# An attention and SoLU kernel on one core: the beginning re-ordered, with a mask from one-input operations and mask products of its own

## The chip, the cores and the metric

The kernel runs on one core of one Trainium2 chip. A core has TensorE (PE, matrix products into PSUM), VectorE (DVE), ScalarE (ACT) and GpSimd (POOL) as compute engines, SyncE (SP) as a queue that issues most transfers, and 16 DMA engines. The metric is the device time of one execution in microseconds, and the median over several runs is compared.

## The reference, cut to what matters

Block-sparse attention (4 batches, 8 heads, 768 tokens, 64 per head; blocks of 32, so 24 blocks) followed by a layer with a SoLU activation:

```python
scores = q @ k.T / sqrt(64)
mask = (|blk_i - blk_j| <= 1) | first and last block row and column
mask[block qb, block kb] = True  for kb in sampled_blocks[qb]      # 3 per row
attn = softmax(where(mask, scores, -1e9))
x = (attn @ v) as [3072 tokens, 512]
h = x @ w_in                                                      # 512 -> 1024
s = h * softmax(h)
out = ((s - mean(s)) / sqrt(var(s) + 1e-6) * g_ln) @ w_out        # 1024 -> 512
```

All inputs are float32 (the block numbers are int64).

## The kernel before, in words

**Units and passes.** The attention goes in 12 passes: 4 batches times 3 thirds of the queries (256 queries each). A pass has 12 units, for 4 head pairs times 3 thirds of the keys, 144 units in all. Unit s: `scores` (L357, products L364) writes keys x queries of two heads into a PSUM tile of two banks (pool `p_sco`, two buffers); `exps` (L371) is one ACT exponential of 128x1024 out of it; `outs` (L379, products L388) multiplies with V, with a column of ones for the sum; after the third unit of a pair `normalise` (L395) divides on VectorE into `xb`. Nothing is masked after the product: K and Q carry 24 extra rows below their 64. In KT they hold `selT`, a one where the key lies in that block; in QT they hold the mask row `row_q`, minus 30000 where the query may not see that block. So one product of 88 rows gives the masked score. `mask_rows` (L589) copies these rows into KT or QT for a head pair (24x1536).

**Preparation.** q, k and v come in as float32 (`load`, L296, a staging pool by size: whole pieces, the first two chunks of a Q, its last four chunks with four buffers). `cast` (L311) makes bfloat16, `turn_mm` (L320) transposes on PE, `turn_out` (L333) copies out of PSUM into KT or QT. Batch 0 is prepared while its first pass runs: K whole, Q only its first two chunks (the first pass), then V, then the other four chunks of Q.

**The mask.** VectorE compares the block numbers with an iota, one-input for the first sample (L564), two-input for the others, which take the maximum with the one before (L567), and multiplies with a static mask that six GpSimd selects have made (L544), again two-input (L569). A product with `selT` (L578) spreads it over 768 queries; ACT copies it into the rows of head pair 0 in QT, and `mask_rows` from there into the others.

**The layer.** Of each pass's result, `x_turn` (L411) sends `xb` through a transposing transfer on SP; for each of two 128-token tiles `h_mms` (L416) makes h, `e_exp` (L425) the exponential, `solu`, `stats` and `rstd` the rest, `ln_turn` (L444) a second transposing transfer, `o_mms` (L476) the product with `w_cen_sb`, `scaled` and `store` the output. `w_cen_sb` is w_out times g_ln (`prep_w`, L659, GpSimd) less its column mean (`prep_mean`, L666, products on PE; `prep_cen`, L675, VectorE).

**The order** is written by hand. Everything before the first units is emitted as it stands; the rest goes on a plan, `at(when, fn, ...)`, sorted by `when`, whose integer part is the unit. Every engine and every queue then takes its instructions strictly in the order emitted, and waits at each for what it needs. So `at(15.9, ...)` puts a product on PE between the scores of units 17 and 18; it does not start it at a time. `zeros` (L551) emits products of a zero tile, fillers whose result nobody reads: 8 before the mask, 5 around the transposes, 12 between the first units.

Of the kernel before, what the change touches and what calls it, by code (L numbers as in the profile page):

```python
# [201 lines left out]
def kernel(  # L202
# [68 lines left out]
    w_out_f = fix.tile([128, KF, d_model], FP32, name="w_out_f")  # L271
# [24 lines left out]
    def load(eng, src, b, pr, key, c0=0, c1=NCH):  # L296
        st = a_st.tile([TQ, 2, (c1 - c0) * D], FP32, tag=f"st{c1 - c0}", name=f"st_{key}{b}_{pr}",
                       bufs={NCH: 7, 2: 4, 4: 4}[c1 - c0])
        stage[key, b, pr, c0] = st
        eng.dma_start(  # L300
            out=st.rearrange("p h (c d) -> p h c d", d=D),
            in_=src[b, 2 * pr : 2 * pr + 2].rearrange("h (p c) d -> p h c d", c=NCH)[
                :, :, c0:c1, :])
# [16 lines left out]
    def turn_mm(b, pr, key, pool, c0=0, c1=NCH):  # L320
# [3 lines left out]
        elif pool is p_op:  # L324
            tp = p_op.tile([128, 1024], BF16, tag="op", name=f"tp_{key}{b}_{pr}_{c0}")
        else:
# [29 lines left out]

    def scores(s):  # L357
        ps, b, j, pr, u = unit(s)
        sco = p_sco.tile([TQ, 2, 512], FP32, tag="sco", name=f"sco{s}")
        sco_of[s] = sco  # L360
        for hh in range(2):
            h = 2 * pr + hh
            for kk in range(2):
                nc.tensor.matmul(  # L364
                    sco[:, hh, kk * QW : (kk + 1) * QW],
                    KT[b % 2][0:KR, h * NCH + 2 * u + kk, :],
                    QT[b % 2][0:KR, h * NCH + PC * j : h * NCH + PC * (j + 1), :].rearrange(
                        "p c t -> p (c t)"),
                    start=(kk == 0), stop=(kk == 1))
# [136 lines left out]
    DVE2 = (nc.vector, nc.vector)  # L506

    with tc.manual_schedule():
# [7 lines left out]
        for pr in (1, 2):  # L516
            load(nc.sync, k, 0, pr, "k")
            load(nc.sync, q, 0, pr, "q", 0, 2)
        load(nc.sync, k, 0, 3, "k")
# [4 lines left out]
        stat_m = fix.tile([NB, NB], FP32, name="stat_m")  # L524
        nc.vector.memset(stat_m, 0.0)
        selT = fix.tile([NB, NCH, TQ], BF16, name="selT")
        nc.vector.memset(selT, 1.0)
        mask_l = fix.tile([NB, KR], BF16, name="mask_l")
        nc.vector.memset(mask_l, 0.0)
        for t in VA:  # L530
            nc.vector.memset(t[:, :, :, D : D + 1], 1.0)
# [7 lines left out]
        for fill, base, cm, step in (  # L539
            (NEG, 1, -1, 1), (NEG, 1, 1, -1),  # L540
            (0.0, -1, 1, 0), (0.0, NB - 2, -1, 0),
            (0.0, -1, 0, 1), (0.0, NB - 2, 0, -1),
        ):
            nc.gpsimd.affine_select(out=stat_m, in_=stat_m, compare_op=ALU.is_ge, fill=fill,  # L544
                                    base=base, channel_multiplier=cm, pattern=[[step, NB]])
# [5 lines left out]
        def zeros(n, pool=p_o):  # L551
# [3 lines left out]
            for _ in range(n):  # L555
# [3 lines left out]
        zeros(8)  # L559
# [3 lines left out]
        acc = [fix.tile([NB, NB], FP32, name=f"acc{r}") for r in range(NR)]  # L563
        nc.vector.tensor_scalar(out=acc[0], in0=io_f, scalar1=samp_f[:, 0:1], scalar2=None,  # L564
                                op0=ALU.is_equal)
        for r in range(1, NR):
            nc.vector.scalar_tensor_tensor(out=acc[r], in0=io_f, scalar=samp_f[:, r : r + 1],  # L567
                                           in1=acc[r - 1], op0=ALU.is_equal, op1=ALU.max)
        nc.vector.scalar_tensor_tensor(out=mask_l[:, D:KR], in0=acc[-1], scalar=0.0, in1=stat_m,  # L569
                                       op0=ALU.is_equal, op1=ALU.mult)  # L570
        cast(nc.scalar, 0, 0, "k", 0, 2, 0)
        cast(nc.scalar, 0, 0, "k", 2, NCH, 0)
        cast(nc.scalar, 0, 0, "q", 0, 2, 0)
        turn_mm(0, 0, "k", p_h, 0, 2)
        m_ps = p_sco.tile([TQ, 2, 512], FP32, tag="sco", name="m_ps")
        sel_f = selT.rearrange("p c t -> p (c t)")
        for i in range(2):
            nc.tensor.matmul(m_ps[0:KR, i, 0 : S // 2], mask_l,  # L578
                             sel_f[:, i * (S // 2) : (i + 1) * (S // 2)], start=True, stop=True)
# [4 lines left out]
        def spread(x, n):  # L584
            return x.rearrange("p (o c) -> p o c", o=1).broadcast_to([NB, n, S])

        row_q = QT[0][D:KR, 0:NCH, :].rearrange("p c t -> p (c t)")

        def mask_rows(eng, t, h0):  # L589
            eng.tensor_copy(out=rows(t, h0, h0 + 2),  # L590
                            in_=spread(sel_f if t in KT else row_q, 2))

        mask_rows(nc.gpsimd, KT[0], 2)
        mask_rows(nc.vector, KT[0], 0)
        warm_t = p_sco.tile([128, 2, 512], FP32, tag="sco", name="warm_t")[:, 0, :]
        zeros(1, warm_t)
        turn_mm(0, 0, "k", p_op, 2, NCH)
        zeros(1, warm_t)
        turn_out(0, 0, "k", DVE2, 0, 2)
        for hh in range(2):  # L600
            nc.scalar.copy(
                out=rows(QT[0], hh, hh + 1).rearrange("p o (i c) -> p (o i) c", i=2),
                in_=m_ps[D:KR, :, 0 : S // 2])
        turn_mm(0, 0, "q", p_o, 0, 2)
        zeros(3, warm_t)
        turn_out(0, 0, "q", DVE2, 0, 2)
        turn_out(0, 0, "k", DVE2, 2, NCH)
        mask_rows(nc.vector, QT[0], 2)
        cast(nc.gpsimd, 0, 1, "k")
        cast(nc.gpsimd, 0, 1, "q", 0, 2)  # L610
        scores(0)
        turn_mm(0, 1, "k", p_h)
        scores(1)
        turn_mm(0, 1, "q", p_o, 0, 2)
        turn_out(0, 1, "k", DVE2)
        turn_out(0, 1, "q", DVE2, 0, 2)

# [5 lines left out]
        load(nc.sync, q, 0, 3, "q", 0, 2)  # L623
        load(nc.sync, v, 0, 0, "v")
        for pr in range(1, NP):
            load(nc.sync, v, 0, pr, "v")
        for pr in range(NP):
            at(0.1, load, nc.sync, q, 0, pr, "q", 2, NCH)
# [340 lines left out]
```

## Time and profile before

| what | us |
|---|---|
| median of three runs | 229.55 (227.93 to 232.82) |
| the profiled execution, its own time | 228.12 |
| its span, first to last instruction | 226.1 |
| PE busy | 208.3 (92%) |
| ACT busy | 174.9 (77%) |
| DVE busy | 156.7 (69%) |
| POOL busy | 109.9 (49%) |
| first exponential starts | 10.98 |
| exponential of the second pass's first unit | 25.73 |

The profile is of one execution. Its rows of a timeline give the start, the busy time of all that is merged in the row, the engine, the line of the code, the operation with output and input, the count (x8), and in brackets how long the engine had been idle and what ended that. The mean granted clock of TensorE over the span is 0.991.

### The profile page before, as it was taken

How to read it: one execution, taken by the hardware profiler on the slowest of the kernel's cores; microseconds unless marked ns; L12 is line 12 of the kernel's file. 1: busy time of each engine (PE TensorE's matmuls, PEld its weight loads, DVE VectorE, ACT ScalarE, POOL GpSimd, SP SyncE). 2: the span in 40 equal slices, each digit the busy share in tenths (PEclk: the TensorE clock that was granted, in tenths of full speed). 3: DMA queues.
4: the chain of work that ended last, by engine and by line, in shares of the span. 5: the costliest groups of instructions: out<-in, count | busy, mean ns of one | idle time of the engine just before them, and what ended most of it. 6: DMA issues, size and time to landing. Idle time of an engine off the chain costs nothing.

```text
span 226.1 us, 5902 instructions
## 1 busy us (share of the span) xinstructions
PE 208.3 (92%) x2336; PEld 146.3 (65%) x2375; DVE 156.7 (69%) x355; ACT 174.9 (77%) x205; POOL 109.9 (49%) x152
## 2 busy tenths in 40 slices
PE   6897888979989999999999999999999999999990
PEld 2466775747757667677776766866766676665450
DVE  7797674797877756867865675786775558558780
ACT  4387888677875988987988898798798889876560
POOL 7899976255895333675853516729720000000010
PEclk9999999999999999999999999999999999999996
DMA  6999694429999329949539749659631463327312
GB/s 176 360 331 296 143 260 162 76 38 252 338 190 284 89 67 188 348 65 286 167 74 299 166 77 316 143 49 324 143 96 34 109 96 96 61 78 130 94 46 101
DMA packets 56147, 37.59 MB, mean 166 GB/s; under 512 B 38068, under 2 KB 51636, under 8 KB 56116
## 3 DMA queue, kind: packets, MB, share of 16 engines
q1 hardware_dynamic: 55172, 35.60, 61.2%
q0 software_dynamic: 528, 1.05, 2.5%
q10 hardware_dynamic: 416, 0.52, 0.7%
q8 instruction: 20, 0.33, 0.6%
q14 instruction: 11, 0.09, 0.2%
HBM read 23.07 MB, written 6.29 MB: 130 GB/s over the span
## 4 chain that ended last, share of the span: by engine, by line
PE 74%; DVE 13%; DMA 4%; ACT 3%; issue 2%; POOL 1%; SPq 0%; DVEq 0%; POOLq 0%; ACTq 0%
PE sco L364 24%; PE o L481 14%; PE op L388 14%; PE h L421 14%; DMA xT<-xb 4%; PE tp_q L329 2%; PE tp_k L329 2%; DVE KT L309 1%; DVE w_cen_sb L676 1%; DVE xb L402 1%; ACT exs L375 1%; ACT e L430 1%; DVE stats L456 1%; PE warm_t L556 1%; DVE QT L309 1%
## 5 line engine op out<-in xcount | busy, mean ns | idle before, releaser
L375 ACT ACTIVATE exs<-sco 128x1024 bf16<-128x1024 f32 x144 | 141.7, 1025 | 16.1 <-PE sco L364 13.5
L364 PE MATMUL sco<-QT,KT 88*128 88x256 bf16 x576 | 86.9, 272 | 2.2 <-ACT exs L375 1.4
L364 PEld LDWEIGHTS <-KT 88*128 88x128 bf16 x576 | 55.0, 97 | 33.2 <-issue 6.5
L388 PE MATMUL op<-VA,exs 128*128 128x65 bf16 x1152 | 52.0, 194 | 1.7 <-DVE xb L402 1.6
L388 PEld LDWEIGHTS <-exs 128*128 128x128 bf16 x1152 | 48.8, 97 | 5.2 <-issue 1.4
L421 PE MATMUL h<-w_in_sb,xT 128*128 128x512 bf16 x153 | 49.4, 378 | 2.3 <-DMA xT<-xb 1.4
L474 POOL TENSOR_TENSOR rstd<-vpe,mhalf 128x1 f32<-128x1 f32 x24 | 13.4, 560 | 71.0 <-DVE vpe L472 59.7
L481 PE MATMUL o<-w_cen_sb,lnT 128*128 128x512 bf16 x162 | 43.5, 379 | 2.2 <-DVE pt_q L338 1.4
L430 ACT ACTIVATE e<-h 128x1024 bf16<-128x1024 f32 x22 | 22.5, 1024 | 19.2 <-PE h L421 14.9
L309 POOL COPY KT<-pt_k 64x768 bf16<-64x768 bf16 x24 | 20.1, 836 | 22.3 <-DVE pt_k L338 21.6
L401 DVE RECIPROCAL recip_all<-op 128x4 f32<-128x4 f32 x48 | 8.7, 182 | 30.2 <-PE op L388 29.9
L456 DVE BATCH_NORM_STATS2 stats<-solu 128x6 f32<-128x512 bf16 x46 | 29.4, 680 | 0.0
L442 DVE TENSOR_TENSOR solu<-h,e 128x1024 bf16<-128x1024 f32 x22 | 26.7, 1216 | 1.2 <-ACT e L430 1.2
L481 PEld LDWEIGHTS <-lnT 128*128 128x128 bf16 x176 | 15.8, 97 | 15.1 <-issue 1.5
L309 POOL COPY QT<-pt_q 64x768 bf16<-64x768 bf16 x24 | 20.1, 837 | 5.5 <-DVE pt_q L338 4.1
L492 DVE TENSOR_SCALAR ot<-o,rstd 128x512 f32<-128x512 f32 x20 | 15.0, 751 | 11.0 <-issue 6.8
L402 DVE TENSOR_TENSOR xb<-op,recip_all 128x256 bf16<-128x256 f32 x48 | 20.4, 425 | 1.7
L421 PEld LDWEIGHTS <-xT 128*128 128x128 bf16 x176 | 15.7, 97 | 6.0 <-DMA xT<-xb 2.0
L309 POOL CAST qn<-st_q 128x768 bf16<-128x768 f32 (+2 forms) x19 | 14.0, 748 | 3.1 <-DMA st_q<-in_q_dram 2.8
L309 POOL CAST kn<-st_k 128x768 bf16<-128x768 f32 x15 | 12.7, 846 | 3.1 <-DMA st_k<-in_k_dram 2.3
L338 DVE COPY pt_q<-tp_q 128x768 bf16<-128x768 bf16 x12 | 6.7, 556 | 8.2 <-PE tp_q L329 8.2
L309 POOL CAST VA<-st_v 128x768 bf16<-128x768 f32 x13 | 10.9, 853 | 1.9 <-DMA st_v<-in_v_dram 1.8
(92 smaller groups left out, 156.6 us busy)
## 6 DMA issues: line engine op xcount, KB each, us to landing
st_v<-in_v_dram SPq DMA_DIRECT2D x16, 384.0 KB, 5.8
out_dram<-ot SPq DMA_DIRECT2D x23, 256.0 KB, 3.7
st_k<-in_k_dram SPq DMA_DIRECT2D x15, 384.0 KB, 4.9
st_q<-in_q_dram SPq DMA_DIRECT2D x12, 384.0 KB, 5.0
w_out_f<-in_moe_w_out_dram SPq DMA_DIRECT2D x4, 512.0 KB, 7.8
st_q<-in_q_dram SPq DMA_DIRECT2D x4, 256.0 KB, 6.9
w_in_sb<-in_moe_w_in_dram POOLq DMA_DIRECT2D x1, 1024.0 KB, 13.4
st_q<-in_q_dram SPq DMA_DIRECT2D x4, 128.0 KB, 4.6
```

The costliest lines, as they stand in the source:

```text
L309: eng.tensor_copy(out=o, in_=i)
L364: nc.tensor.matmul(sco[:, hh, kk * QW : (kk + 1) * QW], KT[b % 2][0:KR, h * NCH + 2 * u + kk, :], QT[b % 2][0:KR, h * NCH + PC * j : h * N ...
L375: nc.scalar.activation(out=exs_of[ps, pr][:, u].rearrange("p a b c -> p (a b c)"), in_=sco_of.pop(s).rearrange("p a b -> p (a b)"), func=A ...
L388: nc.tensor.matmul(op[:, hh, ic, :], exs[:, u, hh, kk, ic * TQ : (ic + 1) * TQ], VA[b % 2][:, 2 * pr + hh, 2 * u + kk, :], start=(u == 0 a ...
L402: nc.vector.tensor_tensor(out=xb_of[ps][:, :, 2 * pr * D : 2 * (pr + 1) * D].rearrange("p c (h d) -> p h c d", h=2), in0=op[:, :, :, 0:D], ...
L421: nc.tensor.matmul(h_of[ps, i][:, half, :], xT_of[ps][:, i * KD + c, :], w_in_sb[:, c, half * HF : (half + 1) * HF], start=(c == 0), stop= ...
L430: nc.scalar.activation(out=o, in_=h, func=ACT.Exp, scale=1.0, accum_out=esum_all[:, t : t + 1])
L442: nc.vector.tensor_mul(out=so, in0=h, in1=e)
L456: nc.vector.bn_stats(out=stat_of[ps, i][:, half, :], in_=so[:, half, :])
L474: nc.gpsimd.tensor_tensor(out=rstd_of[ps, i], in0=vpe, in1=mhalf, op=ALU.pow)
L481: nc.tensor.matmul(ops_of[ps, i], lnT_of[ps, i][:, c, :], w_cen_sb[:, c, :], start=(c == 0), stop=(c == KF - 1), skip_group_check=True)
L492: nc.vector.tensor_scalar(out=o, in0=i_, scalar1=r, scalar2=None, op0=ALU.mult)
```

## The change

It rewrites the beginning of the kernel, up to the layer of the second pass.

- The mask: the three comparisons each go with one input into a column of `seen` (24x24x5), whose other two columns are the neighbours (two GpSimd selects) and the first and last block (memsets); a maximum over the five columns, then one product with a per-row factor, again with one tensor input, gives `mask_l`. `row_q` becomes a tile of its own, copied by VectorE out of PSUM in two parts (256, then 512 columns).
- Units 0 to 5 (head pairs 0 and 1 of the first pass): the mask is added by four products of 24 rows (`mask_mms`) into the score tile, and `scores` uses 64 rows there. The mask rows of these pairs are copied later, before the passes that need them, all on VectorE; those of pair 2 in KT go to GpSimd.
- The first casts and transposes: the last four chunks of K of pair 0 are cast by GpSimd, Q's copy out of PSUM goes to ACT; K of pair 1 goes in two parts.
- w_in comes as four float32 loads on SP, and is cast by GpSimd (before: one load on GpSimd's queue that casts on the way). w_out then loads into the same tile, so after those casts. The last four chunks of Q of pair 0 are loaded ahead of V of pair 3, and their staging pool has three buffers.
- The fillers: 6 at first, then 2.
- `outs` of the first pass come one unit later for each pair; the layer of pass 0 two units later and that of pass 1 one unit later, the second tile of both with its h products closer together; the mean products in two steps instead of four; `prep_cen` alternates between VectorE and GpSimd; batch 1 has its own lists of when to load, cast and turn.

```diff
-                       bufs={NCH: 7, 2: 4, 4: 4}[c1 - c0])
+                       bufs={NCH: 7, 2: 4, 4: 3}[c1 - c0])
...
+    def mask_mms(s):
+        ps, b, j, pr, u = unit(s)
+        sco_of[s] = p_sco.tile([TQ, 2, 512], FP32, tag="sco", name=f"sco{s}")
+        for kk in range(2):
+            for hh in range(2):
+                nc.tensor.matmul(
+                    sco_of[s][:, hh, kk * QW : (kk + 1) * QW], selT[:, 2 * u + kk, :],
+                    row_q[:, j * QW : (j + 1) * QW],
+                    start=(kk == 0), stop=False, skip_group_check=True)
...
-        for r in range(1, NR):
-            nc.vector.scalar_tensor_tensor(out=acc[r], in0=io_f, scalar=samp_f[:, r : r + 1],
-                                           in1=acc[r - 1], op0=ALU.is_equal, op1=ALU.max)
-        nc.vector.scalar_tensor_tensor(out=mask_l[:, D:KR], in0=acc[-1], scalar=0.0, in1=stat_m,
-                                       op0=ALU.is_equal, op1=ALU.mult)
+        for r in range(NR):
+            nc.vector.tensor_scalar(out=seen[:, :, r], in0=io_f,
+                                    scalar1=samp_f[:, r : r + 1], scalar2=None,
+                                    op0=ALU.is_equal)
+        any_f = fix.tile([NB, NB], FP32, name="any_f")
+        nc.vector.reduce_max(out=any_f, in_=seen, axis=AX.X)
+        mask_l = fix.tile([NB, NB], BF16, name="mask_l")
+        nc.vector.tensor_scalar(out=mask_l, in0=any_f, scalar1=0.0, scalar2=neg_r,
+                                op0=ALU.is_equal, op1=ALU.mult)
...
         cast(nc.scalar, 0, 0, "k", 0, 2, 0)
-        cast(nc.scalar, 0, 0, "k", 2, NCH, 0)
         cast(nc.scalar, 0, 0, "q", 0, 2, 0)
+        cast(nc.gpsimd, 0, 0, "k", 2, NCH, 0)
...
+        row_mm(0, 0, QW)
+        turn_mm(0, 0, "k", p_o, 0, 2)
         turn_out(0, 0, "k", DVE2, 0, 2)
...
+        turn_mm(0, 0, "q", p_op, 0, 2)
+        turn_out(0, 0, "q", ACT2, 0, 2)
+        mask_mms(0)
+        row_mm(1, QW, S)
+        turn_mm(0, 0, "k", p_sco, 2, NCH)
         turn_out(0, 0, "k", DVE2, 2, NCH)
+        mask_rows(nc.gpsimd, KT[0], 4)
+        scores(0)
...
+        mask_mms(1)
         scores(1)
...
+        for eng, when, t, h0 in (
+            (nc.vector, 0.9, QT[0], 4), (nc.vector, 3.8, KT[0], 6), (nc.vector, 3.85, QT[0], 6),
+            (nc.vector, 7.5, KT[0], 0), (nc.vector, 7.9, QT[0], 0),
+            (nc.vector, 10.0, KT[0], 2), (nc.vector, 11.2, QT[0], 2),
+            (nc.gpsimd, 14.5, KT[1], 0), (nc.vector, 15.4, QT[1], 0),
+            (nc.vector, 16.6, KT[1], 2), (nc.vector, 18.3, QT[1], 2),
+            (nc.vector, 19.9, KT[1], 4), (nc.vector, 21.3, QT[1], 4),
+            (nc.vector, 30.4, KT[1], 6), (nc.vector, 33.4, QT[1], 6),
+        ):
+            at(when, mask_rows, eng, t, h0)
...
-        for n in range(4):
-            at(n + 0.9, zeros, 3, p_op)
+        at(4.9, zeros, 2, p_op)
...
-            nc.gpsimd.dma_start(out=w_in_sb, in_=moe_w_in.rearrange("(c p) f -> p c f", p=128))
+            nc.sync.dma_start(out=w_f[:, c, :], in_=moe_w_in[c * 128 : (c + 1) * 128, :])
...
-        at(2.25, w_load_in)
-        at(9.0, w_load_out, 0, 6)
-        at(12.1, w_load_out, 6, KF)
...
+        for c in range(KD):
+            at(0.2, w_load_in, c)
+            at(12.0 + 0.1 * c, copy, nc.gpsimd, w_in_sb[:, c, :], w_f[:, c, :])
+            at(12.95, w_load_out, c)
         for c in range(KF):
-            at(13.0 + 0.1 * c, prep_w, c)
-            at(23.1 + 0.45 * c, prep_cen, c)
-        for n in range(4):
-            at(19.85 + n, prep_mean, 2 * n, 2 * n + 2)
+            at(16.0 + 0.1 * c, prep_w, c)
+            at(24.1 + 0.4 * (c // 2), prep_cen, (nc.vector, nc.gpsimd)[c % 2], c)
+        at(22.85, prep_mean, 0, 4)
+        at(23.85, prep_mean, 4, 8)
...
+            if 2 <= s < 2 * UP:
+                at(s - 1.22, mask_mms, s)
...
-            lag = max(0, 3 - pr) if ps == 0 else 0
+            lag = 4 - pr if ps == 0 else 0
...
+        b1_load = [15.2, 16.1, 17.0, 17.9, 21.2, 22.1, 27.2, 28.0, 28.8, 29.6, 30.4, 31.2]
+        b1_cast = [22.0, 23.0, 28.2, 29.4, 31.0, 32.2, 35.0, 36.2, 37.4, 38.6, 40.2, 43.2]
...
-            at(b0 - 0.1, x_turn, ps)
+            at(b0 + (0.9 if ps == 0 else -0.1), x_turn, ps)
...
-                hs = b0 + 6 * i
+                hs = b0 + 6 * i + max(0, 2 - ps)
...
+                if ps < 2 and i == PC - 1:
+                    h_at, es = [(hs + 3.9, 0, 2), (hs + 4.85, 2, 5), (hs + 5.86, 5, 8)], hs + 6.5
```

## The prediction

> **What bounds the kernel now.** I read the page first, then a table by stage of PE, VectorE (DVE) and the DMA engines, then the timelines of ScalarE (ACT), VectorE, PE and SyncE (SP) over the first 70 us. The table (stretch, its length, then busy time of PE, PEld, DVE, ACT, POOL; granted clock, DMA share, GB/s):
>
> ```profile
> 0.00:20.00 20.00, 16.44 (x118) 9.69 (x119) 16.32 (x35) 12.12 (x15) 17.27 (x35) 1.00 0.95 295
> 20.00:60.00 40.00, 35.21 (x463) 26.91 (x470) 28.57 (x66) 31.20 (x35) 26.40 (x30) 1.00 0.69 182
> 60.00:200.00 140.00, 137.30 (x1597) 98.94 (x1626) 96.22 (x213) 117.81 (x136) 63.46 (x83) 1.00 0.66 159
> ```
>
> From 60 to 200 us PE is busy 98%: every microsecond by which that stretch begins earlier, with the same PE work left, comes off the end. Before 60 us PE has gaps, and much of its busy time up to 20 us is products of zeros. So the beginning decides, and its clock is the row of softmax exponentials on ACT, one per unit:
>
> ```profile
> 10.98 3.82 ACT L375 ACTIVATE exs<-sco 128x1024 bf16<-128x1024 f32 x4 [1.98 <-PE sco L364]
> 15.32 3.20 ACT L375 ACTIVATE exs<-sco 128x1024 bf16<-128x1024 f32 x3 [0.51 <-PE sco L364]
> 18.77 1.94 ACT L375 ACTIVATE exs<-sco 128x1024 bf16<-128x1024 f32 x2 [0.25 <-PE sco L364]
> 21.91 1.94 ACT L375 ACTIVATE exs<-sco 128x1024 bf16<-128x1024 f32 x2 [1.20 <-PE sco L364]
> 24.25 1.02 ACT L375 ACTIVATE exs<-sco 128x1024 bf16<-128x1024 f32 x1 [0.40 <-PE sco L364]
> 25.73 5.61 ACT L375 ACTIVATE exs<-sco 128x1024 bf16<-128x1024 f32 x6 [0.46 <-PE sco L364]
> 31.89 3.25 ACT L375 ACTIVATE exs<-sco 128x1024 bf16<-128x1024 f32 x3 [0.55 <-PE sco L364]
> ```
>
> Counting: unit 0 starts at 10.98, unit 3 at 13.85, unit 12 (second pass) at 25.73, unit 18 at 31.89. Back to back a unit takes 0.94 to 1.0; here 18 units take 20.9. What holds them is VectorE, gapless from 9.8 to 21 us, with the mask in two roles: building it, and copying it into the 24 extra rows:
>
> ```profile
> 2.98 0.23 DVE L564 TENSOR_SCALAR acc<-io_f,samp_f 24x24 f32<-24x24 f32 x1
> 3.24 1.81 DVE L567 SCALAR_TENSOR_TENSOR acc<-io_f,samp_f,acc 24x24 f32<-24x24 f32 x2
> 5.16 1.41 DVE L569 SCALAR_TENSOR_TENSOR mask_l<-acc,stat_m 24x24 bf16<-24x24 f32 x1
> ...
> 13.13 0.55 DVE L590 COPY KT<-selT 24x1536 bf16<-24x1536 bf16 x1
> 13.70 1.09 DVE L590 COPY QT<-QT 24x1536 bf16<-24x1536 bf16 x1
> 14.82 1.14 DVE L309 COPY KT<-tp_k 64x768 bf16<-64x768 bf16 x2
> 15.99 0.61 DVE L309 COPY QT<-tp_q 64x256 bf16<-64x256 bf16 x2
> 16.63 1.24 DVE L590 COPY KT<-selT 24x1536 bf16<-24x1536 bf16 x1
> ```
>
> One-input 0.23, two-input 0.9 to 1.41, on the same 24x24. After unit 18, PE's two largest single waits are these:
>
> ```profile
> 47.18 1.67 PE L481 MATMUL o<-w_cen_sb,lnT 128*128 128x512 bf16 x6 [1.37 <-DVE pt_q L338]
> ...
> 67.52 0.60 PE L421 MATMUL h<-w_in_sb,xT 128*128 128x512 bf16 x2 [0.78 <-DMA xT<-xb]
> ```
>
> **The change part by part.** *Mask ready.* Three one-input compares at up to 0.23 from 2.98 end at 3.65; the maximum over five columns is not in the trace: between a memset of that size (0.08) and the two-input 0.90, I take 0.25, nearest to the one-input row; the last product 0.23. With hand-overs 4.2, against 6.57. GpSimd loses four of six 24x24 selects (0.26 each), so selT is ready at 4.0, not 5.0: no bound. Six zero products, not eight, end at 3.9.
>
> *Unit 0.* PE runs its 512-column zeros at 0.43 and the first score group at 0.79 for four until 10.8, but six transposes then in 0.50 and the next score group in 0.60: half rate to about 10.6. I keep that. First mask row product 4.25 to 4.65; its copy (256 columns) between the 0.30 of a 64x256 copy and the 0.69 of a 128x512 fp32 one: 0.45, done 5.15. Q goes through ACT now: cast at 4.5 instead of 4.94, since the second K cast moved to GpSimd; two PSUM copies, bounds 0.2 and 0.74 each, taken 0.42: 6.35. The mask products (4 x 0.215) run 5.5 to 6.35; second row product and four transposes to 7.2; scores 0.86. Unit 0 starts at 8.3, 2.7 earlier.
>
> *Units 1 to 17.* New waits: unit 1's mask product takes the PSUM buffer of the K transposes and waits for their copy, which now stands behind the second row copy (0.7): 8.6. Queued behind it on PE are scores 1 and the transposes of pair 1: at half rate 1.7 and 0.6, so VectorE gets pair 1 at 10.6. From there VectorE is the chain, with its new order: K, Q, K copies of pair 1 (0.61+0.61+0.88), 12.7; a mask copy, mean of the nine in the trace 0.80 (0.55 to 1.24), 13.5; pair 2 (1.14+0.61), 15.2; two mask copies, 16.8; pair 3 (1.75), 18.6; normalise 0.64, two mask copies put off for pair 0, normalise, Q of the second pass 0.87: 22.3. Unit 12 at 22.9 (25.73). Then mask, normalise, mask, 0.87: 25.4, unit 15 at 26.0, and at 0.97 a unit ACT's own pace gives unit 18 at 28.9: 3.0 earlier. So the two pairs without mask rows gain little: their four copies come back before unit 15, and GpSimd's copy and ACT's two return as VectorE's. The 24 mask products are 2.6 us of PE at full rate (0.107 each) and take the place of fillers (5+12-2 zeros, 0.43 or 0.21 each): zero on the path, cover the ACT pace, and 2.6 if that were gone.
>
> Batch 1's rows take seven VectorE copies in place of three, 4 x 0.80 more after unit 15; between 20 and 60 us VectorE is 71% busy, so zero; their cover gone, they delay pass 3 by as much.
>
> *Transfers.* The loads of batch 0 are 4.7 MB and land at 0.36 MB/us from 2 us on, K and Q first as before; the late Q halves go behind three V loads. With three buffers instead of four the last half waits for a GpSimd cast (about 15.1). w_in as four SP loads of 0.52 MB (1.45 us each) then lands at 23.4; its four GpSimd casts of 128x1024 lie between 0.83 (128x768) and 1.47 (two of 512), taken 1.1: 25. Queued behind them is w_out's load, whose buffer is the same, and x_turn(0) passes it. PE wants w_in at unit 17.9, some 29.5: 4 us of cover, cost zero. The old GpSimd load landed at 27.7.
>
> *After unit 18.* Idle PE between 32 and 80 us sums to 3.9, of which 0.78 (36 to 38), 1.19 (46 to 48), 0.78 (66 to 68). The layer, two units later, comes to the o products when w_cen is done (its eight subtractions shared with GpSimd, a 128x512 one between its 0.69 scaling and a 1.46 copy): 1.19 goes. Batch 1's last loads come 2.8 units sooner, clear of the third xT transfer: 0.78 goes. The first stays in kind: x_turn(0) leaves at 26.1 (normalise 3), w_out behind it at 27.8, landing 31.8 plus 3 x 1.45 = 36.2, two scalings 0.69: 37.6; PE reaches the second mean products (unit 23.85) at 36.7, waits 0.9. Behind that wait stand the h products of tile 1; ACT has two scores in hand. One h product more is left at unit 18: 0.2. Sum: -1.19 -0.78 -0.78 +0.9 +0.2 = -1.65.
>
> *Sum.* -3.0 -1.65 = -4.65 from the profiled execution, 228.12 us with a span of 226.1 (2.0 lie around it): **223.5 us**. That execution is 0.6% under the median of the three, 229.55.
>
> **The clock, by trace and by page.** The half rate ends after the first stretch of about 3 us in which PE hardly paused (7.4 to 10.4); before it lies a gap of 1.44. The Trainium skill, page "TensorE: Matmul & The Clock Gate", section "Part 1: The HAM clock gate", says that a free-running window of some 3.4 us must be busy before the array leaves half rate. The trace agrees with that, and the rule speaks against this change, which drops fillers and leaves pauses at 3.9, 7.2 and 8.1. By that rule the sum stands if the window that ended near 10.6 still counts as busy; if the new pauses spoil it, rival 1 holds.
>
> **The rivals.** 1. *Half rate lasts to about 14 us.* For it: pauses where fillers stood. Against: at half rate PE has 1.7 us a unit, more than ACT, so it never pauses after 8.6. Units 2 and 3 then cost 0.86 more each; VectorE gets pair 2 some 1.3 to 2 later: 225.2. 2. *The weights come late, and it ends slower.* POOL's queue holds 17 casts and copies ahead of w_in's, and PE waits in order at unit 17.9. The point is 29.5 us for w_in, from which each microsecond counts; beyond 34 the kernel is slower than before. For it: two GpSimd casts in the trace took 1.12 and 1.14 instead of 0.83. Against: 25 is far off; all 17 casts would need that and half as much again. With w_out behind it, about 230. 3. *Nothing new waits.* The clock opens by 7.2 (VectorE 0.9 sooner), w_out is in time (0.9), and GpSimd leaves the mask copies at 0.65 (1.2 over eight): 220.5. That the mask products relieve VectorE of nothing is mostly true already, and in the sum: the early start is theirs, the chain behind it isn't shorter.
>
> **How the numbers follow.** Forecast 0.55, rival 1 0.20, rival 2 0.10, rival 3 0.15. The range 219.5 to 228.5 reaches from rival 3 with its eight mask copies at the shortest, 0.55 (0.8 less, rounded), to 228.12 - 1.0 + 0.9 + 0.2 = 228.2, where only 1 us of unit 18's lead is left, no old wait goes and the new one comes; it leaves out rival 2 and a bit of rival 3. The forecast's own range is 221.5 to 226. About 2% is what a measurement of this kernel tells from no change; 2% under 229.55 is 225.0. Faster: three quarters of the forecast, rival 3, a little of rival 1: 0.57. Slower: rival 2 almost alone: 0.09. Within: 0.34.
>
> **What would show it.** mask_l done near 4.2; unit 0 near 8.3, unit 12 near 22.9, unit 18 near 28.9; VectorE gapless from 10.6 to 25; no PE wait at the first o products nor at the third xT; one of about 0.9 at the mean products. Score groups still at 0.79 after 11 us would mean rival 1; a PE wait at the first h product for GpSimd, rival 2. If unit 18 is early and the end is not, PE work or waits after it were misjudged.

## The result and the profile after

| | us |
|---|---|
| median, four runs after | 246.0 (244.3 to 250.5) |
| median, four runs before beside them | 228.7 (227.3 to 232.8) |
| ratio | 1.072 (95% interval 1.066 to 1.079) |
| profiled execution after, its span | 246.7, 244.8 |

The forecast was 223.5, with a range to 228.5: the kernel became 7% slower instead of 2.6% faster. Ratios here and below leave out executions in a slower state of the chip, so they are not the quotients of the medians. The table by stage (stretch, its length, busy time of PE, PEld, DVE, ACT, POOL; granted clock, DMA share, GB/s), now of the kernel after:

```profile
0.00:20.00 20.00, 15.46 (x70) 7.13 (x71) 12.21 (x33) 6.88 (x9) 15.97 (x32) 0.69 0.89 293
20.00:60.00 40.00, 34.94 (x409) 25.89 (x412) 27.53 (x59) 28.29 (x31) 20.92 (x24) 0.86 0.57 164
60.00:200.00 140.00, 131.44 (x1502) 93.83 (x1527) 93.11 (x202) 109.19 (x127) 70.55 (x91) 0.99 0.61 159
```

Two things stand out. One is the clock column, 0.69 and 0.86 where the table before has 1.00. (The records of the clock begin at 4.1 us here and only at 10.5 us before, and the column counts what lies ahead of them as 1.00; by their 512-column zero products, one in 0.43 us, both kernels run at half rate there.) The other is PE at 131 instead of 137 us in the long stretch that was 98% busy. The softmax exponentials on ScalarE, timeline of the kernel after:

```profile
11.04 1.02 ACT L389 ACTIVATE exs<-sco 128x1024 bf16<-128x1024 f32 x1 [2.33 <-PE sco L378]
13.07 1.02 ACT L389 ACTIVATE exs<-sco 128x1024 bf16<-128x1024 f32 x1 [1.01 <-PE sco L378]
...
32.44 1.94 ACT L389 ACTIVATE exs<-sco 128x1024 bf16<-128x1024 f32 x2 [0.27 <-PE sco L378]
```

Unit 0 starts at 11.04 as before, unit 12 at 32.4 instead of 25.7. Followed to the end, by the start of each single exponential in the two profiled executions:

| unit | 0 | 12 | 18 | 24 | 36 | 48 | last |
|---|---|---|---|---|---|---|---|
| before | 11.0 | 25.7 | 31.9 | 40.2 | 58.8 | 77.1 | 207.3 |
| after | 11.0 | 32.4 | 39.0 | 46.3 | 68.8 | 95.1 | 225.5 |
| lost so far | 0 | 6.7 | 7.1 | 6.1 | 10.0 | 18.0 | 18.2 |

So there are two losses: some 6 us before unit 24, and 12.0 between units 24 and 48 (48.8 us instead of 36.9). From unit 48 on both kernels go alike.

**The beginning.** The three compares, VectorE's timeline after:

```profile
3.44 2.91 DVE L584 TENSOR_SCALAR seen<-io_f,samp_f 24x24 f32<-24x24 f32 x3
6.45 0.27 DVE L588 TENSOR_REDUCE any_f<-seen 24x24 f32<-24x120 f32 x1
6.75 0.38 DVE L590 TENSOR_SCALAR mask_l<-any_f,neg_r 24x24 bf16<-24x24 f32 x1
```

In order of time they take 1.39, 0.23 and 1.47 us, and the first starts at 3.44 instead of 2.98. GpSimd's timeline in the same microseconds:

```profile
2.44 1.78 POOL L567 TENSOR_SCALAR_AFFINE_SELECT selT<-selT 24x768 bf16<-24x768 bf16 x2
4.18 0.60 POOL L309 CAST kn<-st_k 128x512 bf16<-128x512 f32 x1
4.84 1.46 POOL L613 COPY KT<-selT 24x1536 bf16<-24x1536 bf16 x1
```

The first compare ends at 4.82, just behind the GpSimd cast (4.78), and the third at 6.35, just behind the GpSimd copy (6.30). A one-input compare that meets a running GpSimd operation ends just behind it, like the two-input one; in E9, with GpSimd idle, the second and third take 0.23 each. The Trainium skill, page "SBUF — State Buffer", section "Who interferes with whom", lists `tensor_scalar` among the operations that can take the port pair shared with GpSimd when their operands meet its conditions; the trace agrees.

PE waits for the mask, and its clock closes at 7.5 us. Its first product behind the mask, then the table by stage of PE alone, after (busy time, granted clock, DMA share, GB/s):

```profile
7.19 0.28 PE L604 MATMUL m_ps<-selT,mask_l 24*24 24x256 bf16 x1 [3.07 <-DVE mask_l L590]
```

```profile
4.00:8.00 4.00, 0.88 (x7) 0.94 1.02 319
8.00:12.00 4.00, 3.96 (x17) 0.50 1.06 372
12.00:16.00 4.00, 4.00 (x22) 0.50 0.96 305
16.00:20.00 4.00, 4.00 (x22) 0.50 0.92 320
20.00:24.00 4.00, 4.00 (x22) 0.50 0.62 245
24.00:28.00 4.00, 3.78 (x35) 0.50 0.00 0
```

From 8 to 24 us PE does not pause, yet it runs at half rate until 28 us.

**The weights.** SyncE's timeline after:

```profile
35.89 1.36 SPq L427 DMA_TRANSPOSE xT<-xb  x1
37.31 0.56 SPq L675 DMA_DIRECT2D g_ln_sb<-in_moe_g_ln_dram  x1
37.98 2.10 SPq L676 DMA_DIRECT2D w_f<-in_moe_w_out_dram  x4
```

w_out's loads stand at 12.95, `x_turn(0)` at 12.9: the queue holds them until 37.3, while w_in was cast long before. The groups of GpSimd between 27 and 60 us show what follows, a wait of 15.3 us and centring subtractions of 1.28 us each:

```profile
L681 POOL TENSOR_SCALAR w_out_sb<-w_f,g_ln_sb 128x512 bf16<-128x512 f32 x8 | 5.7, 726 | 15.5 <-DMA w_f<-in_moe_w_out_dram 15.3
L698 POOL TENSOR_TENSOR w_cen_sb<-w_out_sb,mean_sb 128x512 bf16<-128x512 bf16 x4 | 5.0, 1284 | 0.0
```

VectorE's share of these subtractions is as slow beside them: three take 3.55 us, the one ahead of them took 0.41. A copy of turned K stands behind them, and PE waits 2.66 us for it:

```profile
51.33 3.55 DVE L698 TENSOR_TENSOR w_cen_sb<-w_out_sb,mean_sb 128x512 bf16<-128x512 bf16 x3
```

```profile
55.41 0.80 PE L331 MATMUL tp_q<-ident,qn 128*128 128x128 bf16 x6 [2.66 <-DVE pt_k L340]
```

The clock then falls to half from 55.3 to 58.7 us, and once more from 69.0 to 72.4, both between units 24 and 48. At half rate 3.41 us hold half the work, so each fall costs up to 1.7 us (an estimate).

### The profile page after: what moved, and what is told of

It is laid out like the page before. It is cut to its first block, busy times and chain, and to the rows that moved or that the text cites. A ratio compares the mean times of both kernels' runs of the same rounds, so it can differ in the third digit from the quotient of the medians.

```text
span 244.8 us, 5932 instructions
## 1 busy us (share of the span) xinstructions
PE 219.2 (90%) x2346; PEld 150.5 (61%) x2382; DVE 159.9 (65%) x363; ACT 173.4 (71%) x204; POOL 111.3 (45%) x153
## 4 chain that ended last, share of the span: by engine, by line
PE 72%; DVE 12%; DMA 4%; issue 3%; POOL 3%; ACT 2%; SPq 1%; DVEq 0%; POOLq 0%; ACTq 0%
PE sco L378 24%; PE o L495 14%; PE op L402 13%; PE h L435 12%; PE tp_k L331 3%; PE sco L364 2%; PE tp_q L331 2%; DMA w_f<-in_moe_w_out_dram 2%; DMA lnT<-solu 2%; POOL w_out_sb L681 2%; DVE w_cen_sb L698 2%; DVE solu L456 1%; ACT e L444 1%; DVE xb L416 1%; DVE seen L584 1%
## 5 line engine op out<-in xcount | busy, mean ns | idle before, releaser
L378 PE MATMUL sco<-QT,KT 88*128 88x256 bf16 (+1 forms) x576 | 91.3, 282 | 5.6 <-ACT exs L389 4.7
L378 PEld LDWEIGHTS <-KT 88*128 88x128 bf16 (+1 forms) x576 | 55.8, 100 | 37.8 <-issue 12.6
L402 PE MATMUL op<-VA,exs 128*128 128x65 bf16 x1152 | 53.0, 195 | 0.9 <-DVE xb L416 0.8
L402 PEld LDWEIGHTS <-exs 128*128 128x128 bf16 x1152 | 49.8, 99 | 4.9 <-PE sco L378 1.3
L495 PE MATMUL o<-w_cen_sb,lnT 128*128 128x512 bf16 x162 | 44.5, 388 | 2.3 <-DVE pt_k L340 1.3
L435 PEld LDWEIGHTS <-xT 128*128 128x128 bf16 x176 | 15.8, 98 | 5.7 <-issue 1.3
L309 POOL CAST qn<-st_q 128x768 bf16<-128x768 f32 (+2 forms) x19 | 14.3, 753 | 2.8 <-DMA st_q<-in_q_dram 2.6
L309 POOL CAST kn<-st_k 128x768 bf16<-128x768 f32 (+2 forms) x17 | 13.1, 773 | 2.7 <-DMA st_k<-in_k_dram 2.4
L331 PE MATMUL tp_q<-ident,qn 128*128 128x128 bf16 x96 | 9.4, 231 | 3.7 <-DVE pt_k L340 2.7
L681 POOL TENSOR_SCALAR w_out_sb<-w_f,g_ln_sb 128x512 bf16<-128x512 f32 x8 | 5.7, 726 | 15.5 <-DMA w_f<-in_moe_w_out_dram 15.3
```

Source lines behind the costliest of these rows:

```text
L309: eng.tensor_copy(out=o, in_=i)
L331: nc.tensor.matmul(tp[:, c * TQ : (c + 1) * TQ], src[:, pr, c, :], ident, is_transpose=True, start=(c == c0), stop=(c == c1 - 1))
L378: nc.tensor.matmul(sco[:, hh, kk * QW : (kk + 1) * QW], KT[b % 2][0:rows, h * NCH + 2 * u + kk, :], QT[b % 2][0:rows, h * NCH + PC * j : h ...
L402: nc.tensor.matmul(op[:, hh, ic, :], exs[:, u, hh, kk, ic * TQ : (ic + 1) * TQ], VA[b % 2][:, 2 * pr + hh, 2 * u + kk, :], start=(u == 0 a ...
L435: nc.tensor.matmul(h_of[ps, i][:, half, :], xT_of[ps][:, i * KD + c, :], w_in_sb[:, c, half * HF : (half + 1) * HF], start=(c == 0), stop= ...
L495: nc.tensor.matmul(ops_of[ps, i], lnT_of[ps, i][:, c, :], w_cen_sb[:, c, :], start=(c == 0), stop=(c == KF - 1), skip_group_check=True)
```

## The experiments

Eighteen kernels in six groups; each group shared its runs of the kernel before (medians 228.2 to 230.0). Of one kernel, executions differ by up to 3%, so unit times, each from one execution, bear differences of several us and not of one. In several traces the record of the granted clock begins only 15 to 27 us into the span and the column shows 1.00 until then; there the rate is read from the score products, 0.41 us each at half rate and 0.27 at full. The expectations give 37.2 us for units 24 to 48 before and 11.7 for what the change lost there, from rows in which exponentials were merged; single starts give 36.9 and 12.0, and are used throughout.

### First group: the beginning and the order on SP

**E1, more fillers.** `zeros(6)` becomes `zeros(14)`.

> The changed kernel with 14 products of zeros ahead of the mask in place of 6, so that TensorE has no pause until the mask is there; nothing else. Theory 'clock': the granted clock fell to 0.50 at 7.6 us because TensorE stood idle for 3.07 us, and products of 24 and 64 rows don't bring it back; with the pause filled it stays at 1.00 from 8 us on, a group of four mask or score products takes 0.60 and not 1.03, unit 18 starts at 29 to 31 us instead of 39.2, and all that hangs on it comes 8 to 10 us sooner: 228 to 234 us. Rival 'weights': the loss between units 24 and 48 (11.7 us) comes from w_out's load behind the first xT transfer and does not depend on the clock: unit 18 improves as above, but the end only by about as much, 236 to 239 us. Rival 'the clock is only a record': score groups still take 1.03 until 28 us, 245 to 247 us.

Measured: 245.8, ratio 1.065 (1.054 to 1.077); unit 0 at 9.0, unit 12 at 30.3. PE by stage in E1:

```profile
4.00:8.00 4.00, 3.38 (x19) 1.00 0.97 316
8.00:12.00 4.00, 3.33 (x28) 0.88 1.06 376
12.00:16.00 4.00, 4.00 (x22) 0.50 0.85 281
16.00:20.00 4.00, 4.00 (x19) 0.50 1.01 331
```

The clock was open to 11.0 us. It closed behind 3.41 us in which PE was 80% busy, and stayed at half to 24.7 us, with PE 100% busy to 21.3, mostly on products of 24 and 64 rows. So the missing fillers ahead of the mask are not the cause by themselves.

**E2, w_out first.** `at(12.95, w_load_out, c)` becomes `at(12.35, ...)`.

> The changed kernel with w_out's load emitted ahead of the first xT transfer instead of behind it (12.35 in the plan, not 12.95). Theory 'weights': GpSimd stands idle for 15 us because these loads wait behind the transfer on SP; they then leave at about 25 us instead of 38, the scalings are done by 33 instead of 48, and units 24 to 48 lose 2 to 4 us instead of 11.7: 236 to 239 us, with the clock still at 0.50 from 8 to 28 us. Theory 'clock' alone: the first 20 us are the cause, the rest follows from them: 243 to 247 us.

Measured: 243.6, 1.064 (1.057 to 1.071). GpSimd's long wait is gone, and units 24 to 48 still take 48.2 us. Some 2 us of the gain lie ahead of unit 24 (44.4 instead of 46.3), where full rate came at 24.7 instead of 28 us and w_out isn't in use yet: between units 24 and 48 the late w_out itself cost about 0.65 us.

**E3, full rows.** The separate mask products get 128 rows; two ScalarE copies fill row_q with zeros first, so the added rows change nothing:

```diff
-        selT = fix.tile([NB, NCH, TQ], BF16, name="selT")
+        selT = fix.tile([128, NCH, TQ], BF16, name="selT")
-        row_q = fix.tile([NB, S], BF16, name="row_q")
+        row_q = fix.tile([128, S], BF16, name="row_q")
```

> The changed kernel with the mask products at 128 rows (selT and row_q padded with zeros) instead of 24; the 64-row scores and the pause stay, and two short copies on ScalarE write the zeros. Theory 'rows': products that use few rows of the array don't count as work for the clock, and half of TensorE's products now use all 128: the clock returns to 1.00 between 11 and 18 us instead of at 28; unit 18 at 32 to 36 us; 236 to 243 us. Rival 'time': something else keeps the clock at 0.50 for 20 us: as the changed kernel, 245 to 248 us.

Measured: 242.6, 1.050 (1.038 to 1.061). PE by stage in E3:

```profile
8.00:12.00 4.00, 3.89 (x19) 0.50 1.06 373
12.00:16.00 4.00, 4.00 (x29) 0.71 0.95 304
16.00:20.00 4.00, 3.92 (x38) 1.00 0.93 347
```

Full rate from 14.3 us instead of 28, unit 12 at 26.4 instead of 32.4, as theory 'rows' gave it; units 24 to 48 still 50.0.

**E4, the kernel before without its 17 later fillers.**

> The kernel before without its later fillers (the five among the first transposes and the twelve between the first units; the eight at the start stay). Theory 'clock': these fillers are what opens the clock at about 10.6 us; without them the first units run at half rate, 0.79 to 1.0 a group, for 5 us or more: unit 12 later than 25.73 by 1 to 6 us, 230 to 236 us. Rival 'fillers don't matter': 88-row scores open it anyway, 227.5 to 230 us.

Measured: 230.2, 1.007 (1.003 to 1.010). Unit 0 at 7.8, unit 12 at 24.6, unit 18 at 31.8 as before. The clock was open from 5.6 us on without these fillers, but from 15.8 to 19.2 us PE was 45% busy, and then the rate was half to 22.6: what unit 0 gains is gone by unit 18. Neither expectation had that course.

### Second group: units 24 to 48

All four have w_out first and all `prep_cen` on VectorE.

**E5, centring on VectorE.** `(nc.vector, nc.gpsimd)[c % 2]` becomes `nc.vector`.

> The change with w_out's loads ahead of the x_turn of pass 0 (as in the run before, 243.6 us, units 24 to 48 in 48.2 us) and with all eight centred products prep_cen on VectorE. Theory G (the four prep_cen on GpSimd, 1.25 us each, lock VectorE out and so delay the turned tiles that TensorE waits for): units 24 to 48 take 43 to 45 us and the time is 239 to 240. Theory P (the o products no longer stand just behind the next tile's e exponential, so TensorE and ScalarE wait for one another in turn) and theory B (the second batch's loads, casts and turns at their new times): units 24 to 48 still take 46.5 to 48, the time is 242 to 243.

Measured: 243.5, 1.062 (1.049 to 1.075); units 24 to 48 in 47.0. Theory G is worth about a microsecond there, and nothing that shows in the time.

**E6, the late part at its times of before.** In E5: `hs = b0 + 6 * i`, five h steps everywhere, and batch 1, mean and centring at their old numbers.

> As the kernel of all prep_cen on VectorE, and besides the layer of passes 0 and 1 (five h steps, no shift), the loads, casts and turns of batch 1, and the mean and centring steps at their times of before; the beginning up to unit 12 stays changed. Theories P and B: units 24 to 48 go back to 38 to 41 us, so the time is 234 to 237. If only the late mask, the slow clock and the late w_out of the beginning cost time, they stay at 46 to 48 and the time is 241 to 243.

Measured: 237.3, 1.034 (1.022 to 1.046); units 24 to 48 in 39.8 us, with one fall of the clock among them (78.1 to 81.5).

**E7, only the o products.** In E5:

```diff
                 os = hs + (12 if ps == LP - 2 and i == PC - 1 else 14)
+                os = {(0, 1): 33.0, (1, 0): 37.0, (1, 1): 44.0}.get((ps, i), os)
```

> As the kernel of all prep_cen on VectorE, with only the o products of (0,1), (1,0), (1,1) put 0.34 unit behind the next e exponential again (33.84, 37.84, 44.84 in place of 34.84, 39.84, 45.84; two turns of batch 1 make room). Theory P: units 24 to 48 take 39 to 43 us, the time is 235 to 238. Theory B: no gain, 46 to 48 us and 241 to 243.

Measured: 237.6, 1.038 (1.026 to 1.050); units 24 to 48 in 40.9 us, with no fall of the clock (E5 has one, 76.7 to 80.1). The runs of E5 (242.7 to 247.3) and E7 (236.7 to 239.9) do not overlap. Three numbers in the plan (and two turns of batch 1 that make room, by 0.6 and 0.1 unit) are worth 5.9 us. The waits between 60 and 100 us in E5 (total, times, longest), of PE and then of ACT:

```profile
PE sco L378 <- ACT exs L389: 3.9, 3, 1.7
```

```profile
ACT exs L389 <- PE sco L378: 9.8, 6, 4.5
ACT e L444 <- PE h L435: 5.4, 4, 2.2
```

and the same in E7:

```profile
PE sco L378 <- ACT exs L389: 0.2, 1, 0.2
```

```profile
ACT e L444 <- PE h L435: 6.2, 5, 2.0
ACT exs L389 <- PE sco L378: 3.3, 5, 1.6
```

Beside the 12 score exponentials of a pass ScalarE has two e, 1.02 us each. During an e PE soon has no free score buffer. Before, the o products of another tile (seven by the plan; a row of six takes 1.67 us) stood 0.34 unit behind each e and filled that time. The change moved the four e of passes 0 and 1 by 2, 0, 1 and -1 units and their o by 2, 2, 1 and 1. Now PE waits for ACT at each e, and one or two units later ACT waits for PE, which does o with no e beside it. Both orders have the same work.

**E8, E6 with full rows.**

> As the kernel with the late part at its times of before, and besides the separate mask products padded with zeros to 128 rows (selT and row_q). If few-row products keep the granted clock at half, it opens near 14 us in place of 28, units up to 18 end 3 to 4 us sooner, and the time is 2 to 4 us under that kernel's: 231 to 234. If the beginning's time is set by the mask and GpSimd alone, both are within 1 us.

Measured: 235.3 (232.0 to 236.4; E6 235.9 to 239.1). Full rate from 14.3, unit 12 at 27.1; then PE idles for 1.6 us in 24 to 28 and the clock is half for about 7 us.

### Third group: the mask and VectorE's copies

**E9, E8 with GpSimd kept off the compares.** The cast of chunks 2 to 5 of K of pair 0 goes to ScalarE, the GpSimd mask rows behind the casts of pair 1.

> The kernel with the late part at its times of before and 128-row mask products (235.3 us, mask_l ready at 6.5, unit 0 at 10.4, unit 12 at 27.1), and besides GpSimd kept off the compares: the cast of k's chunks 2 to 5 of pair 0 on ScalarE, and the KT mask rows of pair 2 behind the casts of pair 1. Theory L (each compare waits for the end of the GpSimd operation that runs): mask_l ready at 5.0 to 5.7, unit 0 at 9.2 to 9.8. If the mask's lateness reaches the end, the time is 234 to 234.6; if units up to 12 are bound by later work on VectorE and the loads, unit 12 stays at 26.5 to 27.5 and the time at 235, plus or minus 1. If the compares are slow in themselves, mask_l stays at 6.4.

Measured: 236.4 (233.8 to 236.9). mask_l ready at 5.19, the compares 1.11 in all, unit 0 at 9.5, as expected; but half rate to 24 us, unit 12 at 29.7, and no gain.

**E10, E8 with the mask rows of pairs 0 and 1 early,** ahead of GpSimd's casts of w_in.

> The same kernel of 235.3 us, and besides the mask rows of pairs 0 and 1 copied on VectorE before GpSimd's casts of w_in (two at once behind pair 0's turns, two at 2.5 and 2.6, in place of 7.5 to 11.2, where they take 1.35 us instead of 0.55 beside those casts and hold up the normalise steps). Theory: TensorE's idle time from 24 to 28 us (1.6 us) shrinks to under 0.8, the granted clock does not fall near 28, unit 24 starts at 42 to 43 in place of 44.9, and the time is 231.5 to 233.5. Rival: the copies only delay the first turns on VectorE, unit 12 starts 1 to 2 us later and the time is 235 to 236.

Measured: 233.6 (232.4 to 236.5), 1.022 (1.013 to 1.032); unit 24 at 43.5, no fall of the clock at 28. Both lie just outside what was expected, and the ranges of E8 and E10 overlap. Its compares tell something by chance, on VectorE:

```profile
3.45 1.11 DVE L584 TENSOR_SCALAR seen<-io_f,samp_f 24x24 f32<-24x24 f32 x3
```

and on GpSimd:

```profile
4.40 0.63 POOL L309 CAST kn<-st_k 128x512 bf16<-128x512 f32 x1 [0.16 <-DMA st_k<-in_k_dram]
5.09 1.46 POOL L615 COPY KT<-selT 24x1536 bf16<-24x1536 bf16 x1
```

Behind its selects GpSimd waited 0.16 us for K and began the cast at 4.40 instead of 4.18. In that pause the second and third compare ran, and the last was through at 4.56: mask_l at 5.19 instead of 7.13, with the same order of code up to there.

**E11, both edits.**

> Both edits at once. If both theories hold and add up: unit 0 at 9.2 to 9.8, unit 24 at 41.5 to 42.5, 230.5 to 233 us, that is 0.5 to 2% above before. If the clock still falls once near 28 or 34 us: 234 to 235.

Measured: 237.2 (234.0 to 238.1). In its trace PE waits 3.4 us at the first h products, and a new fall of the clock follows. They do not add up.

**E12, the kernel before with the one-input mask alone.**

> The kernel before with one part of the change alone: the mask from one-input compares, reduce_max and one product, with two small selects on GpSimd in place of six. Theory L: the compares still wait for GpSimd's selT selects and KT mask rows, mask_l is ready at 5.5 to 6.3 (6.57 before) and only because GpSimd has four selects fewer; unit 0 starts 0 to 1 us sooner and the time is within 0.7% of before. Rival (one-input compares escape GpSimd): mask_l at 4.2 to 4.7, unit 0 near 9.0; the time still within 1%, since unit 18 kept its time when unit 0 started 3.2 us sooner without the fillers.

Measured: 231.6, 1.013 (1.006 to 1.020): a rise, which neither theory gave. mask_l is ready at 6.41. VectorE and then PE in E12:

```profile
14.02 1.90 DVE L593 COPY QT<-QT 24x1536 bf16<-24x1536 bf16 x1
```

```profile
22.17 0.66 PE L388 MATMUL op<-VA,exs 128*128 128x65 bf16 x16 [1.93 <-DVE xb L402]
```

The copy that took 1.09 takes 1.90. GpSimd, four selects lighter, reaches its casts 0.8 us sooner and runs beside other VectorE copies; normalise is late, PE idles 1.93 us (1.17 before), and the clock is half from 24.4 to 27.8 us. Unit 18 starts at 34.1 instead of 31.9.

### Last groups: what was still open

**E13, E12 with GpSimd's old timing.** The two selects run twice: `for sg in (1, -1, 1, -1)`.

> The kernel before with the one-input mask alone (231.6 us, unit 12 at 28.3), and GpSimd's two small selects on seen done twice, which changes no value and gives GpSimd's later work its time of before (selT's selects from about 3.25 us). Theory F (the 3 us came only from GpSimd's work running 0.8 us sooner beside VectorE's mask copies, which then hold up the normalise steps, idle TensorE for 1.9 us at 20 us and bring the clock down at 24): unit 12 starts at 25.5 to 26.5, no half rate at 24 to 28, the time is 228 to 229.5. Rival (the compares cost it): unit 12 at 27.5 or later, 230.5 to 232.

Measured: 229.6 (227.9 to 232.6, twelve runs), 1.005 (1.001 to 1.008). The median is 1.0 us above that of the kernel before, in place of 3.4. But its profiled execution (230.8) still has half rate at 21 to 25 us and unit 12 at 27.1, against the expectation. It speaks for GpSimd's timing without settling it: the intervals of E12 and E13 overlap.

**E14, E10 with outs and x_turn of pass 0 a unit sooner,** and the two fillers 0.2 unit sooner.

> The kernel of 233.6 us (late part at its times of before, 128-row mask products, early mask rows), and besides the outs products of pass 0 one unit sooner (lag 3, 2, 1, 0 in place of 4, 3, 2, 1) and the x_turn of pass 0 at 11.9 in place of 12.9, as before the change. If the unit of lag is what still holds the first h products, unit 18 starts at 33.3 to 34.3 in place of 35.1, xT is not waited for, and the time is 231.5 to 232.8. If it is the beginning up to unit 12 (27.1 against 25.7 before) and the copies on VectorE, the time stays at 233 to 234.5.

Measured: 238.4 (237.8 to 238.8), 1.043 (1.039 to 1.047), worse than E10: half rate to 27 us though the mask products have 128 rows, unit 12 at 32.0. What the lag is worth is hidden by that.

**E15 and E16, E6 without separate mask products,** all scores of 88 rows, without and with 12 fillers.

> The kernel with w_out first, centring on VectorE and the late part at its times of before (237.3 us, half rate to about 26 us, unit 12 at 31.6), with the separate mask products undone: pairs 0 and 1 get their mask rows into KT[0] and QT[0] on VectorE at the beginning, so all scores are of 88 rows, and no product of 24 or 64 rows is left but the two that expand the mask. Theory R (products of few rows do not count for the clock, and there are 48 more of them in pass 0): full rate by 14 to 18 us, unit 0 at 10.5 to 12 but unit 12 at 26 to 28, 231 to 234.5 us. Rival (the clock stays at half whatever the rows, because TensorE pauses for the mask at the beginning): half rate until 24 or later, unit 12 at 30 or later, 236 to 238.

> The same, with three zero products of 128 rows behind each of the first four units, as the kernel before has them. Theory R: full rate by 11 to 14 us, unit 12 at 25.5 to 27.5, 230 to 233.5 us. Rival: half rate until 24 or later, 236 to 238.

Measured: 238.2, 1.043 (1.035 to 1.051), and 234.9, 1.021 (1.013 to 1.028). Half rate to about 27 and 21 us, so theory R as I put it fell: here PE pauses (2.66 us twice in E15, for mask rows in QT), and what it does in a given time is again too little to open the clock (worked out at the end of the next section).

**E17, the kernel before with three o products one unit later.**

> The kernel before, with only the o products of tiles (0,1), (1,0) and (1,1) one unit later (33.84, 39.84, 45.84 in place of 32.84, 38.84, 44.84; two turns 0.05 later to make room), so that they stand 1.34 instead of 0.34 unit behind the next tile's e exponential. Theory P: TensorE waits for ScalarE at those exponentials and ScalarE for TensorE at the o products, units 24 to 48 take 40 to 44 us instead of 37.2, and the time is 231.5 to 235. Rival (the loss between units 24 and 48 needs the rest of the shift too): 36.5 to 38.5 us, the time within 0.7% of before.

Measured: 232.4, 1.019 (1.007 to 1.030); units 24 to 48 in 42.0 instead of 36.9. (Unit 24 itself starts 1.2 us sooner than before, behind a mask that was ready early.) PE's waits between 40 and 80 us in E17:

```profile
PE sco L364 <- ACT exs L375: 4.3, 3, 1.4
PE o L481 <- DVE pt_q L338: 1.4, 1, 1.4
```

The first line does not exist in the kernel before: three waits of 1.4 us, one per moved group of products, are 4.3 of the 5.1 us. With E7 this is the mechanism shown both ways.

**E18, the mended pieces together,** E7 with full rows and early mask rows.

> The pieces together: w_out first, centring on VectorE, the o products of passes 0 and 1 realigned with the layer left in its shifted place (237.6 us alone), mask products of 128 rows, early mask rows. If they add up as with the late part at its old times (237.3 to 233.6): 233 to 235, and not below before, since unit 12 cannot start before 26.5.

Measured: 233.7 (231.1 to 236.1), 1.013 (1.000 to 1.026), with unit 24 at 44.2 and 41.0 us to unit 48. The profiled execution is its slowest (236.1), at half rate to 24.7 us. No variant ran below the kernel before.

## Why the prediction was wrong, step by step

*Units 24 to 48: the largest error.* The step "After unit 18 ... Sum: -1.19 -0.78 -0.78 +0.9 +0.2 = -1.65" priced waits one by one where the layer moved, and took ScalarE's e and PE's o products as loads without a place. They had one: o filled the time in which PE cannot go on because of e. Measured from unit 18 on: +11.1 us in the place of -1.65, and +12.0 between units 24 and 48. Of these 12.0, 6.2 are the pairing (47.0 to 40.9, E5 to E7; 5.9 in the time), the fall of the clock in E5 included; 1.8 are the late w_out and the centring on GpSimd (48.8 to 47.0). The rest, 40.9 against 36.9, seems to belong almost wholly to the other times of the late part: E9 and E16, which have all of it at its old times and no fall of the clock there, take 37.5 and 37.4. Which of those times it is wasn't taken apart. The price of an o wait that should go stayed too, only elsewhere; PE's timeline after:

```profile
81.45 1.67 PE L495 MATMUL o<-w_cen_sb,lnT 128*128 128x512 bf16 x6 [1.25 <-DVE pt_k L340]
```

The wait of h for xT (0.78) did go.

*Mask ready at 4.2.* It was 7.13, and 6.3 to 6.5 in E1, E2, E5 and E7, which have the same mask code. The compares took 2.91 us in place of 0.67, and began 0.46 later. The step "Three one-input compares at up to 0.23" took as the price one row in which the compare began between two GpSimd selects. The trace before held the pattern, by GpSimd's timeline:

```profile
3.24 1.78 POOL L547 TENSOR_SCALAR_AFFINE_SELECT selT<-selT 24x768 bf16<-24x768 bf16 x2
5.08 1.46 POOL L590 COPY KT<-selT 24x1536 bf16<-24x1536 bf16 x1
```

There the two-input compares ended at 5.05, where GpSimd's selects ended (5.02), and mask_l at 6.57, where its copy of the KT rows ended (6.54). The maximum was right, 0.27 for 0.25.

*Half rate to 10.6, "I keep that".* It stayed to 28. This step carried over the moment at which the clock opened before, though the products ahead of it had changed from mostly 128 rows to mostly 24 and 64. "At half rate PE has 1.7 us a unit ... so it never pauses" came true, and did not open the clock. "From there VectorE is the chain" failed with it: from 10.6 to 25 us VectorE was busy for 6.6 us of 14.4, and PE at half rate was the chain, 1.8 us a unit. Units 0 to 12 cost 21.4 us instead of 14.7. Rival 1 had the long half rate, but for another reason (pauses) and far too short; it ended at 14 by assumption.

*Unit 18 at 28.9.* It was 39.0. Besides the above, little of a gain at unit 0 reaches unit 18: E4 starts unit 0 3.2 us sooner, at 7.8, and E17, whose beginning is that of the kernel before, by chance at 8.2 (its mask was ready at 5.0); unit 18 starts at 31.8 and 30.7 against 31.9.

*w_in in time.* Right: PE waits nowhere for it. *x_turn(0) at 26.1, w_out at 27.8*: 35.9 and 38.0, late by the 10 us that the units were late; the order was foreseen. The wait at the mean products was 0.3, not 0.9.

*The other side.* I gave slower 0.09, almost all of it to a late w_in. The chance hung on one place, when nearly every wait of a hand-set plan was moved.

*What opens the clock.* The Trainium skill, page "TensorE: Matmul & The Clock Gate", section "Part 1: The HAM clock gate", has it open after about 3.4 us of busy time; here 16 us of 100% busy PE left it at half, so busy time alone isn't the measure. E3 shows that the rows of the products matter. The kept traces say more. In each of them the recorded changes of the clock lie whole multiples of 3.41 us apart. Take the stretches of 3.41 us that this grid gives, and count every product in a stretch by its columns times its rows over 128 (24*128 24x256 is 24 rows and 256 columns; a product that crosses an end counts by its share of time). For instance, nearly all of the products from 14.35 to 17.76 us in the kernel after are these:

```profile
L378 PE MATMUL sco<-QT,KT 64*128 64x256 bf16 x8 | 2.1, 410 | 0.0
L364 PE MATMUL sco<-row_q,selT 24*128 24x256 bf16 x7 | 1.9, 413 | 0.0
```

| kernel | stretch, us | PE busy | sum | the clock behind it |
|---|---|---|---|---|
| before | 7.12 to 10.53 | 100% | 3618 | opens |
| before | 17.36 to 20.77 | 66% | 4058 | stays full |
| after | 14.35 to 17.76 | 100% | 1304 | stays half |
| after | 24.59 to 28.00 | 100% | 3340 | opens |
| E1 | 7.62 to 11.03 | 80% | 2423 | closes |
| E3 | 10.91 to 14.33 | 100% | 3129 | opens |
| E9 | 10.41 to 13.83 | 100% | 2934 | stays half |
| E12 | 20.98 to 24.40 | 54% | 2987 | closes |

In the 20 traces the full rate ended behind 28 such stretches, none with more than 3055, and went on behind 1201, none with less than 3084. At half rate (ahead of the first record taken as half) 70 stretches left it so, none with more than 3032, and 43 opened it, none with less than 3003 but two: in these (2747 in E2, 2761 in E1) the record of a planned product of 512 columns is missing. So in these traces the border lies between some 3000 and 3080, whether PE pauses or is busy with few rows. E9, E14 and E18 have mask products of 128 rows like E3, but their stretches stay at 2946 and below up to 20 us or later. This was worked out afterwards from the traces; no run was made to test it.

*Open.* Some 3 to 5 us between the best variants and the kernel before are not assigned to one cause. In E10's trace 1.4 us are lost by unit 12, 1.9 more by unit 18 and 1.2 between units 24 and 48.

## What to carry to other kernels

In a hand-set order, look which engine's work fills which other engine's wait, and move such pairs together: three groups of products one unit off cost 5.1 us of units 24 to 48, and 1.9% of the time, with not one instruction more. Price an operation by its slowest rows beside the neighbour it will have, not by its best row. A gain at the start of a chain is worth nothing until the next units are shown to start earlier too. Where products get fewer rows, do not carry over the moment at which the clock opened.

## What the runs showed of the hardware that was not expected

- TensorE's granted clock stayed at half for 14 us (E1) and 20 us (after), with PE 94% busy or more, most of the time with products of 24 and 64 rows; 256-column products took 0.41 instead of 0.27 us. With PE 66% busy on products of 88 and 128 rows it stayed at full (before, 17.4 to 20.8 us). Columns times rows in stretches of 3.41 us tell the two apart.
- A 24x24 one-input compare takes 0.23 us alone and up to 1.47 beside GpSimd; a transfer landing some 0.2 us later gave a mask 2 us sooner (E10).
- Beside GpSimd's subtractions, VectorE's of the same size took 1.18 us each instead of 0.41 (after).
- The kernel before with the one-input mask and four fewer selects on GpSimd (0.26 us apart) was 1.3% slower (E12); a copy on VectorE took 1.90 us instead of 1.09. E13 speaks for GpSimd's timing as the cause without settling it.
